# VectorE's share in two more chunks, other parts for chunks 1 and 2, and the transposes of K inside the first PV batch

## The chip, the core and the metric

One core of a Trainium2 chip. The metric is the device time of one launch in microseconds. The kernel before takes 521.86 us (median of three runs, 521.71 to 523.05). For every run the span of the core is known too (first to last counted event of the trace); the time is somewhat longer than the span (by 1.67 us in the profiled run of before). One run of each kernel is profiled.

## The reference

Grouped-query attention with softmax, bf16: 16 batches, 32 query heads, 8 key heads, 288 queries, 512 keys, width 128.

```python
k = jnp.repeat(k, rep, axis=1); v = jnp.repeat(v, rep, axis=1)      # rep = 4
scores = jnp.einsum("bhqd,bhkd->bhqk", q, k) * D ** -0.5
p = softmax(scores); out = jnp.einsum("bhqk,bhkd->bhqd", p, v)
```

## The kernel before

There are 128 groups (batch and key head). The scores of a group, 128 keys x 4608 columns, are cut into three chunks of 1536 columns, 384 chunks in all. TensorE computes the scores of chunk n into one of two PSUM buffers, ScalarE takes exp of them into bf16, and TensorE multiplies by V two chunks later, in a batch of 12 small matmuls (PV); a column of ones in V gives the softmax sum. VectorE takes the reciprocal and evicts. In every sixth chunk VectorE exponentiates 120 of the 1536 columns itself, with a bit trick and a polynomial ("share"). The order on the engines (cut):

```python
FIRST = 2; FIRST_SHARED = 6; EVERY = 6; LAG = 2; TPC = 3

def shared(n):
    return FIRST_SHARED <= n < NS - NC and (n - FIRST_SHARED) % EVERY == 0    # 63 chunks: 6, 12 ... 378

def op_exp(n):                        # ScalarE
    parts = [(0, CH)]
    if shared(n): parts = [(0, CH - W)]                      # 1416 columns
    if n < FIRST or n == NS - 1:
        parts = [(x, x + BANK) for x in range(0, CH, BANK)]  # three times 512
    ...

# TensorE
op_warm(WARM, BANK, ps_o[:, 1]); op_warm(1, P, ps_o[:, 1])   # matmuls on a constant
op_kt(0, range(1), 0); op_kt(0, range(1, NJ), 1)             # K of group 0, transposed
op_warm(1, P, ps_s[:, 1])
for n in range(NS):
    op_s(n)                                                  # scores; wait for K, Q, a free buffer
    if shared(n): op_sy(n)                                   # the 120 columns for VectorE, waits for an eviction
    if n == 2: op_kt(1, range(NJ), 1)                        # K of group 1, transposed
    if n >= LAG: op_pv(n - LAG)

# ScalarE: fetches K of group 1 only when K of group 0 is copied
op_kd(eng, 0); eng.activation(dum[:], ..., ACTF.Exp)
for (s, n) in need(eng, [("s_k0", 2)]): eng.wait_ge(s, n)
op_kd(eng, 1)

# VectorE
op_kc(1, range(NJ), 1, 3)                                    # copies the transposed K; chunk 3 needs it
for r in range(NS - 1):
    n = r + LAG
    op_rc(r)
    if shared(n): op_y(n)
    if shared(n - 1): op_yu(n - 1, 1); op_yu(n - 1, 2); op_yp(n - 1)
    op_ev(r)
    if shared(n): op_yb(n); op_ym(n); op_yu(n, 0)
```

Of the kernel before, what the change touches and what calls it, by code (L numbers as in the profile page):

```python
# [131 lines left out]
def bass_standalone__gqa_softmax__near_ridge_kernel(  # L132
# [13 lines left out]
    NG = B * G  # L146
    assert D == P and Sk % P == 0 and R % P == 0
    BANK = 512
    TPC = 3
    CH = TPC * BANK  # L150
    COLS = NJ * R
    NC = COLS // CH
# [8 lines left out]
    LAG = 2  # L161
    W = 120
    EVERY = 6
# [6 lines left out]
    NQ = 12  # L170
    NPT = 6
    WARM = 5
    FIRST = 2
    FIRST_SHARED = 6
    AHEAD = 1.08
    NO = 12
    NS = NG * NC
    LASTG = NG - 1
    ALONE = 8 * TPC


# [6 lines left out]
    with ExitStack() as es:  # L188
        sem = {}
# [57 lines left out]
        ck_sb = main.enter_context(nc.sbuf_tensor("ck_sb", [P, 3], FP32))  # L247
        bad_sb = main.enter_context(nc.sbuf_tensor("bad_sb", [P, 2, ALONE + 1], FP32))
        y_sb = main.enter_context(nc.sbuf_tensor("y_sb", [P, NB, W], FP32))
# [21 lines left out]
        def emit(eng, waits, fn):  # L271
            waits = need(eng, waits)
            for (s, n) in waits[:-1]:
                eng.wait_ge(s, n)
            ins = fn()
            if waits:
                ins.wait_op(waits[-1][0], waits[-1][1], "sem-ge")
            return ins
# [53 lines left out]
        def op_store(g, i=None):  # L332
            eng = nc.sync
            if i is None:
                for (s, n) in need(eng, [("s_ev", NC * (g + 1))]):
                    eng.wait_ge(s, n)
                eng.dma_start(o_v[g], o_sb[:, g % NO].rearrange("p t d -> p (t d)")).then_inc(
                    sem["s_o%d" % (g % NO) if g < LASTG - 1 else "s_ol"], 16)
            else:
# [6 lines left out]
        def stored():  # L346
            return [("s_o%d" % (g % NO), 16 * (g // NO + 1)) for g in range(NG - NO, LASTG - 1)]

# [21 lines left out]
        def used(i):  # L370

            return max(b for b in range(NC) for t in range(b * TPC, (b + 1) * TPC) for j in range(NJ) if place(t, j)[0] == i)

        def ready(n, x):

            if n < FIRST and x < TPC - 1:
                return ("s_eb", n * (TPC - 1) + x + 1)
            return ("s_e", n + 1 + (x if n == NS - 1 else 0))

        def sequence(b):  # L380

# [17 lines left out]
        def op_kt(g, tiles, bank):  # L399

            eng = nc.tensor
            dst = ps_o[:, bank].bitcast(BF16)
            for x, j in enumerate(tiles):
                ins = emit(eng, [("s_id", 2), ("s_kd%d" % g, 16)], lambda: eng.transpose(  # L404
                    dst[:, x * P:(x + 1) * P], kd_sb[:, g, j * D:(j + 1) * D], ident[:]))
            ins.then_inc(sem["s_kp"], 1)
# [13 lines left out]
        def op_s(n):  # L420
            eng = nc.tensor
            g, i = n // NC, n % NC
            sl, gi = (g // UG) % NSLOT, g % UG
            waits = [have("k", g), have_q(g, i)]
            if n >= 2 + FIRST:
                waits.append(("s_e", n - 1))
            qg = qt_sb[:, g % NQ].rearrange("d t p -> d (t p)")
            todo = pieces(i)
            for x, (c, j, t, w) in enumerate(todo):
                if shared(n) and c + w == CH:  # L430
                    w -= W
                w_x = waits if x == 0 else []
                if n == 0 and x < 2:
                    w_x = [("s_k0", 1), waits[1]] if x == 0 else waits[:1]
                if n == 1 and x < 2:
                    w_x = [have_q(g, x)]
                if 2 <= n < 2 + FIRST:
                    w_x = w_x + [ready(n - 2, c // BANK)]
                ins = emit(eng, w_x, lambda: eng.matmul(  # L439
                    ps_s[:, n % 2, c:c + w], kt_sb[:, sl, j, gi, :], qg[:, t * P:t * P + w], start=True, stop=True))  # L440
                if n < FIRST and (c + w) % BANK == 0 and c + w < CH:
                    ins.then_inc(sem["s_s0"], 1)
            ins.then_inc(sem["s_s"], 1)

# [14 lines left out]
                return ps_s[:, 0, 0:TPC * DV].rearrange("p (a e) -> p a e", e=DV)  # L459
            return ps_o[:, r % 2, 0:TPC * DV].rearrange("p (a e) -> p a e", e=DV)  # L460

        def op_pv(r):
            eng = nc.tensor
            g = r // NC
            sl, gi = (g // UG) % NSLOT, g % UG
            waits = [("s_vc", g + 1)]
            if 2 <= r < NS - 2:
                waits.append(("s_ev", r - 1))
            if r == NS - 2:
                waits.append(("s_e", NS - 1))  # L470


            todo = sequence(r % NC)
            for x, (t, j) in enumerate(todo):
                i, c = place(t, j)
                w_x = (waits if x == 0 else []) + [ready(g * NC + i, c // BANK)]
                if c == CH - P and shared(g * NC + i):
                    w_x.append(("s_yp", nth(g * NC + i)))
                ins = emit(eng, w_x, lambda: eng.matmul(  # L479
                    outs(r)[:, t - r % NC * TPC, :], pt(g, t, j), v_sb[:, sl, gi * NJ + j, 0:DV], start=(x == 0),  # L480
                    stop=(t not in [y[0] for y in todo[x + 1:]]), skip_group_check=True))
            ins.then_inc(sem["s_pv"], 1)

        def op_pv_last():

            eng = nc.tensor
            sl, gi = (LASTG // UG) % NSLOT, LASTG % UG
            for (x, j) in [(x, j) for j in range(NJ) for x in range(TPC - 1)] + [(TPC - 1, j) for j in range(NJ)]:
                t = NT - TPC + x
                i, c = place(t, j)  # L490
                w_x = [ready(LASTG * NC + i, c // BANK)] + ([ready(NS - 1, 0)] if x == TPC - 1 else [])
                ins = emit(eng, w_x, lambda: eng.matmul(
                    outs(NS - 1)[:, x, :], pt(LASTG, t, j),
                    v_sb[:, sl, gi * NJ + j, 0:DV], start=(j == 0), stop=(j == NJ - 1)))
# [3 lines left out]
        def op_exp(n):  # L498
            eng = nc.scalar
            waits = [("s_s", n + 1)]  # L500
            if n >= NPT:
                m = n - NPT
                waits.insert(0, ("s_pv", m // NC * NC + used(m % NC) + 1))
            d, s = pt_sb[:, n % NPT], ps_s[:, n % 2]
            parts = [(0, CH)]
            if shared(n):
                parts = [(0, CH - W)]
            if n < FIRST or n == NS - 1:
                parts = [(x, x + BANK) for x in range(0, CH, BANK)]
            for x, (c, e) in enumerate(parts[:-1]):  # L510
                ins = emit(eng, [("s_s0", (TPC - 1) * n + x + 1)] if n < FIRST else waits, lambda: eng.activation(  # L511
                    d[:, c:e], s[:, c:e], ACTF.Exp, scale=scale))
                ins.then_inc(sem["s_e" if n == NS - 1 else "s_eb"], 1)
            parts = [(d[:, c:e], s[:, c:e]) for (c, e) in parts[-1:]]
            for (d, s) in parts:
                emit(eng, waits, lambda: eng.activation(d, s, ACTF.Exp, scale=scale)).then_inc(sem["s_e"], 1)  # L516


        def shared(n):
            return FIRST_SHARED <= n < NS - NC and (n - FIRST_SHARED) % EVERY == 0  # L520

        def nth(n):
            return (n - FIRST_SHARED) // EVERY + 1

        def op_y(n):
            eng, b = nc.vector, nth(n) % NB
# [63 lines left out]
        def op_ev_last():  # L590

            n, c, t = TPC - 1, TPC * (NS - 1), NT - TPC
            waits = [("s_o%d" % (LASTG % NO), 16 * (LASTG // NO)), ("s_rc", NS)]
            dst, src = o_sb[:, LASTG % NO, t:NT, :], outs(NS - 1)[:, :, 0:D]
# [12 lines left out]
        def op_stat(b):  # L607
            eng = nc.vector
            w = G * NT
            a, e = b * w, (b + 1) * w - (ALONE if b == B - 1 else 0)  # L610
            emit(eng, [("s_rc", e // TPC)], lambda: eng.tensor_reduce(  # L611
# [18 lines left out]
        for u in range(1, NU):  # L630
            t = max(NC * UG * (u - NSLOT + 1) + 0.5, NC * (UG * u - 2.5) / AHEAD - 0.2)
            sp.append((t, lambda u=u: op_k(u)))
            sp.append((t + (2.0 if u >= NSLOT else 0.35), lambda u=u: op_v(u)))
        for g in range(UG, NG):
            t = max(NC * (g - NQ + 1) + 1.2, NC * (g - 2.5) / AHEAD)
# [16 lines left out]
        @block.tensor  # L652
        def _(eng):
            op_warm(WARM, BANK, ps_o[:, 1])
            op_warm(1, P, ps_o[:, 1])
            op_kt(0, range(1), 0)
            op_kt(0, range(1, NJ), 1)
            op_warm(1, P, ps_s[:, 1])
            for n in range(NS):
                op_s(n)  # L660
                if shared(n):
                    op_sy(n)
                if n == 2:
                    op_kt(1, range(NJ), 1)
                if n >= LAG:
                    op_pv(n - LAG)
            op_pv(NS - 2)
            op_pv_last()
            emit(eng, [("s_ev", NS - 2), ("s_bad", 2)], lambda: eng.matmul(  # L669
                ps_o[0:1, NS % 2, 0:ALONE + 1], one_f[:], bad_sb[:, 1, :], start=True, stop=True)  # L670
            ).then_inc(sem["s_bad"], 1)
            choose(eng, "pe")
# [25 lines left out]
        def _(eng):  # L698
# [4 lines left out]
            per_b = G * NC  # L703
            w0 = NS - 1 - ALONE // TPC
            last = rl_sb[:, NG * NT - ALONE:NG * NT]
# [61 lines left out]
```

## Time and profile before

| | before |
|---|---|
| time, span | 521.67 us, 520.0 us (profiled run) |
| TensorE, ScalarE, VectorE, GpSimd busy | 98%, 99%, 71%, 15% |
| a chunk in the steady part | 1.330 us |
| scores of chunk 0, 3, 7 and 383 start at | 4.41, 8.31, 13.76, 513.99 us |

TensorE's matmul records overlap (the three of one chunk's scores at 17.75 fill 0.81 us, and the batch after them starts 0.65 later), so starts are compared here, not busy times. A chunk's pace is the same from chunk 7 to the end. The lines that carry this are in the prediction. In the profile lines, PE is TensorE's matmuls, PEld its weight loads, DVE VectorE, ACT ScalarE and POOL GpSimd.

### The profile page before, as it was taken

The numbers are of one execution on the slowest core, as the hardware profiler recorded it, in microseconds if no ns is written. First come the engines' busy times: TensorE is split into PE (matmuls) and PEld (weight loads), VectorE is DVE, ScalarE is ACT, GpSimd is POOL, SyncE is SP. The second block draws the span as 40 slices with busy tenths as digits, with TensorE's granted clock in tenths as the row PEclk, the third lists the DMA queues.
The fourth block names the chain that finished last, engine by engine and source line by source line (L and its number), as shares of the span: only waits on it lengthen the run. The fifth ranks groups of instructions, "written<-read, shape, count | busy, mean of one in ns | idle before, by whom it ended". The sixth has DMA issues, their size and how long they took to land.

```text
span 520.0 us, 15243 instructions
## 1 busy us (share of the span) xinstructions
PE 510.3 (98%) x6118; PEld 394.6 (76%) x6224; DVE 369.6 (71%) x1315; ACT 513.3 (99%) x393; POOL 79.8 (15%) x135
## 2 busy tenths in 40 slices
PE   8999999999999999999999999999999999999997
PEld 5777777777777777777777777777777777777776
DVE  2767767777777677676776776767767767677776
ACT  7999999999999999999999999999999999999997
POOL 2111111111111111111111111111111111111110
PEclk9999999999999999999999999999999999999999
DMA  9999999999999998999999989999998989998212
GB/s 186 237 218 230 267 194 248 225 213 210 219 233 256 208 245 201 235 248 240 215 241 209 209 225 220 241 185 209 229 240 232 227 194 201 192 234 198 86 69 93
DMA packets 253078, 110.06 MB, mean 212 GB/s; under 512 B 219728, under 2 KB 236752, under 8 KB 253008
## 3 DMA queue, kind: packets, MB, share of 16 engines
q1 hardware_dynamic: 252720, 108.82, 97.7%
q8 instruction: 49, 0.80, 0.7%
q10 hardware_dynamic: 288, 0.26, 0.2%
q14 instruction: 21, 0.17, 0.2%
HBM read 17.04 MB, written 37.75 MB: 105 GB/s over the span
## 4 chain that ended last, share of the span: by engine, by line
ACT 98%; DMA 1%; issue 1%; DVE 0%; PE 0%
ACT pt_sb L516 97%; DMA qt_sb<-in_q_dram 1%; ACT pt_sb L511 1%; PE ps_s L439 0%; DVE o_sb L585 0%; DVE o_sb L595 0%; PE ps_s L479 0%; DVE rl_sb L575 0%; PE ps_o L669 0%; DVE bad_sb L621 0%; DVE flag_i L734 0%; DVE bad_sb L618 0%
## 5 line engine op out<-in xcount | busy, mean ns | idle before, releaser
L516 ACT ACTIVATE pt_sb<-ps_s 128x1536 bf16<-128x1536 f32 (+2 forms) x384 | 508.8, 1441 | 0.0
L479 PE MATMUL ps_o<-v_sb,pt_sb 128*128 128x129 bf16 x4584 | 322.3, 220 | 1.1
L479 PEld LDWEIGHTS ps_o<-v_sb,pt_sb 128*128 128x128 bf16 x4584 | 282.8, 98 | 49.7 <-DVE o_sb L585 14.1
L439 PE MATMUL ps_s<-qt_sb,kt_sb 128*128 128x512 bf16 (+2 forms) x1430 | 290.4, 320 | 5.0 <-DMA qt_sb<-in_q_dram 0.5
L585 DVE TENSOR_TENSOR o_sb<-ps_o,rl_sb 128x384 bf16<-128x384 f32 x382 | 211.9, 555 | 9.3 <-DVE rl_sb L575 0.5
L439 PEld LDWEIGHTS ps_s<-qt_sb,kt_sb 128*128 128x128 bf16 x1536 | 123.9, 98 | 62.3 <-issue 1.1
L575 DVE RECIPROCAL rl_sb<-ps_o 128x3 f32<-128x3 f32 x382 | 68.1, 178 | 125.5 <-PE ps_o L479 124.0
L568 POOL COPY v_sb<-vd_sb 128x512 bf16<-128x512 bf16 x128 | 78.8, 616 | 429.1 <-PE ps_o L479 408.9
L549 DVE SCALAR_TENSOR_TENSOR u_sb<-u_sb,m_sb 128x120 f32<-128x120 f32 x126 | 35.6, 283 | 2.2
L556 DVE SCALAR_TENSOR_TENSOR pt_sb<-u_sb,e_sb 128x120 bf16<-128x120 f32 x63 | 17.8, 283 | 2.2
L549 DVE SCALAR_TENSOR_TENSOR u_sb<-m_sb 128x120 f32<-128x120 f32 x63 | 17.4, 277 | 0.0
L527 DVE TENSOR_SCALAR y_sb<-ps_o 128x120 f32<-128x120 f32 x63 | 15.9, 253 | 0.0
L540 DVE TENSOR_SCALAR m_sb<-t_sb 128x120 int32<-128x120 int32 x63 | 14.1, 223 | 2.2
L540 DVE TENSOR_SCALAR e_sb<-t_sb 128x120 int32<-128x120 int32 x63 | 13.6, 216 | 0.0
L450 PE MATMUL ps_o<-qt_sb,kt_sb 128*128 128x120 bf16 x63 | 13.6, 216 | 0.0
L533 DVE TENSOR_SCALAR t_sb<-y_sb 128x120 int32<-128x120 f32 x63 | 13.4, 213 | 0.0
L450 PEld LDWEIGHTS ps_o<-qt_sb,kt_sb 128*128 128x128 bf16 x63 | 6.2, 98 | 7.4
L511 ACT ACTIVATE pt_sb<-ps_s 128x512 bf16<-128x512 f32 x6 | 3.3, 616 | 2.3 <-PE ps_s L439 2.3
L411 DVE COPY kt_sb<-ps_o 128x128 bf16<-128x128 bf16 (+2 forms) x3 | 1.0, 336 | 6.2 <-PE ps_o L404 6.1
L613 DVE TENSOR_REDUCE st_sb<-rl_sb 128x1 f32<-128x72 f32 (+1 forms) x16 | 3.5, 216 | 0.0
L611 DVE TENSOR_REDUCE st_sb<-rl_sb 128x1 f32<-128x72 f32 (+1 forms) x16 | 3.5, 216 | 0.0
L417 PE MATMUL ps_o<-const-bfloat16-1.0 128*128 128x512 bf16 (+1 forms) x6 | 2.4, 570 | 0.9 <-PEq L752 0.9
(32 smaller groups left out, 12.0 us busy)
## 6 DMA issues: line engine op xcount, KB each, us to landing
out_dram<-o_sb SPq DMA_DIRECT2D x127, 288.0 KB, 3.7
vd_sb<-in_v_dram SPq DMA_DIRECT2D x31, 512.0 KB, 5.5
qt_sb<-in_q_dram SPq DMA_TRANSPOSE x128, 4.9
kt_sb<-in_k_dram SPq DMA_TRANSPOSE x32, 5.1
vd_sb<-in_v_dram SPq DMA_DIRECT2D x1, 384.0 KB, 4.6
out_dram<-o_sb SPq DMA_DIRECT2D x3, 96.0 KB, 1.6
kd_sb<-in_k_dram ACTq DMA_DIRECT2D x2, 128.0 KB, 2.7
vd_sb<-in_v_dram SPq DMA_DIRECT2D x1, 128.0 KB, 3.3
```

What stands on the lines that cost most here:

```text
L439: ins = emit(eng, w_x, lambda: eng.matmul(ps_s[:, n % 2, c:c + w], kt_sb[:, sl, j, gi, :], qg[:, t * P:t * P + w], start=True, stop=True))
L450: emit(eng, [("s_ev", n - LAG - 1)], lambda: eng.matmul(ps_o[:, (n - LAG) % 2, BANK - W:BANK], kt_sb[:, (g // UG) % NSLOT, j, g % UG, :], ...
L479: ins = emit(eng, w_x, lambda: eng.matmul(outs(r)[:, t - r % NC * TPC, :], pt(g, t, j), v_sb[:, sl, gi * NJ + j, 0:DV], start=(x == 0), st ...
L516: emit(eng, waits, lambda: eng.activation(d, s, ACTF.Exp, scale=scale)).then_inc(sem["s_e"], 1)
L527: emit(eng, [("s_yb", nth(n) - NB), ("s_pv", n - LAG + 1)], lambda: eng.tensor_scalar(out=y_sb[:, b], in0=ps_o[:, (n - LAG) % 2, BANK - W: ...
L533: emit(eng, [("s_ym", 2 * (nth(n) - NB)), ("s_y", nth(n))], lambda: eng.tensor_scalar(out=t_sb[:, b], in0=y_sb[:, b], scalar1=Y_MUL, scala ...
L540: emit(eng, [("s_yp", nth(n) - NB), ("s_yb", nth(n))], lambda: eng.tensor_scalar(out=dst[:, b], in0=t_sb[:, b], scalar1=mask, scalar2=bits ...
L549: lambda: eng.scalar_tensor_tensor(out=u_sb[:, b, x], in0=src, scalar=QUARTIC[x], in1=m, op0=ALU.add, op1=ALU.mult)
L556: lambda: eng.scalar_tensor_tensor(out=pt_sb[:, n % NPT, CH - W:CH], in0=u_sb[:, b, 2], scalar=QUARTIC[3], in1=e_sb[:, b].bitcast(FP32), o ...
L568: emit(eng, waits, lambda: eng.tensor_copy(v_sb[:, sl, gi * NJ:(gi + 1) * NJ, 0:D], vd_sb[:, sl, gi].rearrange("p (j d) -> p j d", d=D))). ...
L575: emit(eng, [("s_pv", r + 1)], lambda: eng.reciprocal(rl_sb[:, TPC * r:TPC * (r + 1)].unsqueeze(2), outs(r)[:, :, D:DV])).then_inc(sem["s_ ...
L585: emit(eng, waits, lambda: eng.tensor_tensor(out=o_sb[:, g % NO, t0:t0 + TPC, :], in0=outs(r)[:, :, 0:D], in1=rl_sb[:, TPC * r:TPC * (r + ...
```

## The change

Its intent: relieve ScalarE by two more shares (chunks 3 and 381), let work that depends on part of chunk 2 start sooner, and fill the wait for K of group 1 with PV matmuls.

```diff
-    FIRST = 2
-    FIRST_SHARED = 6
+    FIRST = 3
+    PARTS = {0: (1, 2, 3), 1: (2, 3), 2: (2, 3), NG * NC - 1: (1, 2, 3)}
+    SHARED = [NC] + list(range(2 * NC, NS - NC, EVERY)) + [NS - NC]
 ...
-        def op_pv(r):
+        def op_pv(r, some=slice(None)):
 ...
-            parts = [(x, x + BANK) for x in range(0, CH, BANK)]
+            parts = [(x * BANK, y * BANK) for (x, y) in zip((0,) + PARTS[n], PARTS[n])]
 ...
-            return FIRST_SHARED <= n < NS - NC and (n - FIRST_SHARED) % EVERY == 0
+            return n in SHARED
 ...
                 if n == 2:
+                    op_pv(0, slice(0, TPC * TPC))
                     op_kt(1, range(NJ), 1)
-                if n >= LAG:
+                elif n == 3:
+                    op_pv(0, slice(TPC * TPC, None))
+                    op_pv(1)
+                elif n > 3:
                     op_pv(n - LAG)
```

More of the change, by code (lines that the diff above doesn't have):

```diff
@@ L372, in used, with part, ahead @@
             return max(b for b in range(NC) for t in range(b * TPC, (b + 1) * TPC) for j in range(NJ) if place(t, j)[0] == i)
+        def part(n, x):
+            return sum(x >= e for e in PARTS.get(n, (TPC,)))
+        def ahead(n):
+            return sum(len(PARTS[m]) - 1 for m in range(n))
         def ready(n, x):
-            if n < FIRST and x < TPC - 1:
-                return ("s_eb", n * (TPC - 1) + x + 1)
-            return ("s_e", n + 1 + (x if n == NS - 1 else 0))
+            p = part(n, x)
+            if n < FIRST and p < len(PARTS[n]) - 1:
+                return ("s_eb", ahead(n) + p + 1)
+            return ("s_e", n + 1 + (p if n == NS - 1 else 0))
         def sequence(b):
@@ L440, in op_s @@
                     ps_s[:, n % 2, c:c + w], kt_sb[:, sl, j, gi, :], qg[:, t * P:t * P + w], start=True, stop=True))
-                if n < FIRST and (c + w) % BANK == 0 and c + w < CH:
+                if n < FIRST and (c + w) % BANK == 0 and (c + w) // BANK in PARTS[n][:-1]:
                     ins.then_inc(sem["s_s0"], 1)
@@ L473, in op_pv @@
             todo = sequence(r % NC)
-            for x, (t, j) in enumerate(todo):
+            for x, (t, j) in list(enumerate(todo))[some]:
                 i, c = place(t, j)
@@ L481, in op_pv @@
                     stop=(t not in [y[0] for y in todo[x + 1:]]), skip_group_check=True))
-            ins.then_inc(sem["s_pv"], 1)
+            if x == len(todo) - 1:
+                ins.then_inc(sem["s_pv"], 1)
         def op_pv_last():
@@ L507, in op_exp @@
                 parts = [(0, CH - W)]
-            if n < FIRST or n == NS - 1:
-                parts = [(x, x + BANK) for x in range(0, CH, BANK)]
+            if n in PARTS:
+                parts = [(x * BANK, y * BANK) for (x, y) in zip((0,) + PARTS[n], PARTS[n])]
             for x, (c, e) in enumerate(parts[:-1]):
-                ins = emit(eng, [("s_s0", (TPC - 1) * n + x + 1)] if n < FIRST else waits, lambda: eng.activation(
+                ins = emit(eng, [("s_s0", ahead(n) + x + 1)] if n < FIRST else waits, lambda: eng.activation(
                     d[:, c:e], s[:, c:e], ACTF.Exp, scale=scale))
@@ L519, in shared @@
         def shared(n):
-            return FIRST_SHARED <= n < NS - NC and (n - FIRST_SHARED) % EVERY == 0
+            return n in SHARED
         def nth(n):
-            return (n - FIRST_SHARED) // EVERY + 1
+            return SHARED.index(n) + 1
         def op_y(n):
```

## The prediction

> **What bounds the kernel now.** I read first the busy times and the chain that ended last.
>
> ```profile
> PE 510.3 (98%) x6118; PEld 394.6 (76%) x6224; DVE 369.6 (71%) x1315; ACT 513.3 (99%) x393; POOL 79.8 (15%) x135
> ...
> ACT 98%; DMA 1%; issue 1%; DVE 0%; PE 0%
> ```
>
> TensorE and ScalarE are both full; the chain names ScalarE alone. That would make every column taken off ScalarE a gain, so I checked it with the timeline of ScalarE, one instruction at a time (start, duration), in the steady part. Chunk 12 (1416 columns, VectorE does the other 120) and its neighbours:
>
> ```profile
> 19.95 1.48 ACT L516 ACTIVATE pt_sb<-ps_s 128x1536 bf16<-128x1536 f32 x1
> 21.28 1.39 ACT L516 ACTIVATE pt_sb<-ps_s 128x1416 bf16<-128x1416 f32 x1
> 22.59 1.45 ACT L516 ACTIVATE pt_sb<-ps_s 128x1536 bf16<-128x1536 f32 x1
> 23.94 1.45 ACT L516 ACTIVATE pt_sb<-ps_s 128x1536 bf16<-128x1536 f32 x1
> ```
>
> Ends are 21.43, 22.67, 24.04, 25.39. A backlogged full chunk costs about 1.344 us (ends of chunks 2 to 5: 9.44, 10.78, 12.12, 13.47) and a shared one 1.24. But chunk 13 ends 1.37 after chunk 12: ScalarE had caught up and waited a little for scores, which the records hide because consecutive ones overlap. So in the steady part ScalarE is fed by TensorE. The timeline of TensorE confirms it (L439 scores of a chunk, L479 its PV batch, L450 VectorE's scores):
>
> ```profile
> 17.75 0.81 PE L439 MATMUL ps_s<-qt_sb,kt_sb 128*128 128x512 bf16 x3
> 18.40 0.84 PE L479 MATMUL ps_o<-v_sb,pt_sb 128*128 128x129 bf16 x12
> ...
> 19.73 0.84 PE L479 MATMUL ps_o<-v_sb,pt_sb 128*128 128x129 bf16 x12
> 20.41 0.76 PE L439 MATMUL ps_s<-qt_sb,kt_sb 128*128 128x512 bf16 x3
> 21.01 0.22 PE L450 MATMUL ps_o<-qt_sb,kt_sb 128*128 128x120 bf16 x1
> 21.06 0.84 PE L479 MATMUL ps_o<-v_sb,pt_sb 128*128 128x129 bf16 x12
> 21.74 0.81 PE L439 MATMUL ps_s<-qt_sb,kt_sb 128*128 128x512 bf16 x3
> ```
>
> Scores take 0.65 us, a batch 0.68, and a chunk starts every 1.33, shared or not. Scores of chunk 13 start at 21.74, though the buffer half they need was free at 21.43 (end of chunk 11's exponential): 0.31 of slack. TensorE waits for nobody. From scores of chunk 7 (13.76) to those of 383 (513.99), 376 chunks take 500.23 us, 1.3304 each; ScalarE alone would need (5 x 1.344 + 1.24) / 6 = 1.327. The two are balanced to 0.003 us a chunk, with TensorE the slower. Hence the end is, nearly, the moment at which TensorE's steady run begins plus a constant. The first 14 us decide.
>
> There I read both rows of TensorE, weight loads (PEld) and matmuls (PE):
>
> ```profile
> 7.30 0.23 PEld L404 LDWEIGHTS ps_o<-ident,kd_sb 128*128 128x128 bf16 x4 [0.16 <-DMA kd_sb<-in_k_dram]
> 7.49 0.72 PEld L479 LDWEIGHTS ps_o<-v_sb,pt_sb 128*128 128x128 bf16 x12
> 8.28 0.34 PEld L439 LDWEIGHTS ps_s<-qt_sb,kt_sb 128*128 128x128 bf16 x3
> ...
> 7.31 0.40 PE L404 MATMUL ps_o<-ident,kd_sb 128*128 128x128 bf16 x4
> 7.54 0.84 PE L479 MATMUL ps_o<-v_sb,pt_sb 128*128 128x129 bf16 x12
> 8.31 0.81 PE L439 MATMUL ps_s<-qt_sb,kt_sb 128*128 128x512 bf16 x3
> 8.96 0.94 PE L479 MATMUL ps_o<-v_sb,pt_sb 128*128 128x129 bf16 x12
> ...
> 7.74 0.42 DVE L411 COPY kt_sb<-ps_o 128x512 bf16<-128x512 bf16 x1 [3.51 <-PE ps_o L404]
> ```
>
> The last matmul of the scores of chunk 2 starts at 7.10 and the next could at 7.15; K of group 1 lands at 7.30, so 0.16 is lost. Batch 0 (12 matmuls at 0.056) should be followed at 8.22 but scores of chunk 3 start at 8.31: they wait for VectorE's copy of the transposed K (7.74 to 8.16, seen at 8.28), 0.09 lost. Batch 1 takes 0.77 instead of 0.68, since its weight load at 9.49 waits for the undivided exponential of chunk 2 (end 9.44): 0.09 lost. Batch 4 (13.04 to 13.76) loses 0.04 in the same way to chunk 5 (end 13.47). In all about 0.38 us that a better start could return at most.
>
> [...] this trace has 0.488 for 512 columns and 1.344 for 1536, so 0.836 a column and 0.06 fixed. [...]
>
> **The change, part by part.**
>
> 1. VectorE takes 120 columns of chunks 3 and 381. ScalarE saves 120 x 0.836 = 0.10 us each. TensorE's work hardly changes: 512 columns become 392 + 120 with one more weight load (scores still take 0.65 in the shared chunks above). So this speeds up only the engine that waits. At the tail, scores of chunk 383 are complete at 513.99 + 0.82 = 514.81 and ScalarE starts on them at 514.87. Its backlog then is 0.02 (0.62 for the first 512 columns where 0.60 is the unqueued value), all that can be gained. Against that, VectorE gets ten more instructions just three chunks after chunk 378's; the score matmul of 381 needs the eviction of batch 377 (ends 511.91) and can slip by some 0.05. I count the tail +0.02.
>
> 2. Parts. Chunk 1 goes from 3 x 512 (3 x 0.488 = 1.464) to 1024 + 512 (0.916 + 0.488 = 1.404): -0.06. Chunk 2 goes from 1.344 to 1.404: +0.06. Together nil on ScalarE. But batch 1 and the scores of chunk 4 can begin when two thirds of chunk 2 are done, at about 8.95 instead of 9.44, so the 0.09 in batch 1 goes, if it is still on the path.
>
> 3. The order on TensorE. Before: scores 2, transposes, 12 PV, scores 3, 12 PV. After: scores 2, 9 PV, transposes, scores 3 with VectorE's share, 3 + 12 PV. The intent is to fill the 0.16 spent waiting for K. [...] But nothing now stands between the transposes and the scores that need their copy. Before, transposes at 7.31 led to scores at 8.31, a lag of 1.00: four issues and the last result 0.43, copy 0.42, semaphore and weight load 0.15. The copy chain is the same, so scores 3 start at 7.66 + 0.99 = 8.65, 0.34 later than before. TensorE idles from 7.89 to 8.65, 0.76 us, in place of 0.16 + 0.09.
>
> The sum on TensorE: after scores 3 come 0.65, 15 PV of 0.845, and scores 4 at 8.65 + 1.49 = 10.14, against 9.73 now (+0.41). Exponential 2 is over at about 9.42, so nothing else is waited for. Scores 7 follow at 10.14 + 3 x 1.33 = 14.13, because the 0.04 of batch 4 goes too (ScalarE is no longer behind); now 13.76. So +0.37 at the start of the steady run, +0.02 at the tail: about +0.35 to +0.4 us on 521.86.
>
> **Rivals.**
>
> A. ScalarE is the bound, as the chain of waits says. Then the change gives -0.2 us (two shares) and some more if the start tightens: 521.6. For it: 99% busy and no idle in its row. Against: the steady 1.33 of TensorE through shared chunks, its 0.31 of slack, and the 1.37 after a shared chunk.
>
> B. The copy is quicker than I think, or K landing is later in runs without a profile, so that the reordering pays. If no wait at all were left, scores 7 would start at 7.15 + 0.23 + 4 x 0.65 + 5 x 0.68 = 13.38, 0.38 earlier: 521.5. For it: an author of a tuned kernel would try this for such a gain. Against: the measured chain of 1.00 us has nothing to lie beside, while the wait it removes was 0.16. A middle case would be near no change.
>
> C. The gap makes TensorE drop to half clock for a while. The first four score matmuls, before the warm state, are spaced 0.42 us instead of 0.215. [...] I give it 4%.
>
> D. VectorE, with shares in chunks 3 and 6, delays a PV batch. After chunk 6's share, eviction 5 ends at 16.91 and batch 7 starts on time at 17.07. Eviction of batch 0 now ends just before batch 1's sums are ready, so I expect at most 0.05.
>
> **Range and chances.** The working gives 522.2. I lean 0.1 towards A and B, since I may have missed what the author saw: 522.1. The three runs of before spread over 1.3 us (521.71 to 523.05), so a median can be off by 0.3. Range 521.45 to 522.75: below it B would have to hold in full, above it C. Nothing here is near 2% (10.4 us): faster 0.01, same 0.98, slower 0.01.
>
> **What would show it.** In the changed profile: the transposes of group 1 at about 7.66 without a wait for their DMA; a gap on TensorE of about 0.75 us before the scores of chunk 3, which start near 8.65 after VectorE's copy ends near 8.5; scores 4 near 10.14; exponentials of chunks 4 to 12 with unqueued durations of 1.45 instead of 1.52; a chunk still every 1.330 us; 65 exponentials of 1416 columns; scores of chunk 383 near 514.35. I am wrong if scores 3 start before 8.4, if TensorE's pace in the steady part changes (then ScalarE did bound it), or if matmuls after the gap are spaced 0.42.

The forecast's sum came to +0.37 us at the start of the steady run and +0.02 at the tail, so 0.35 to 0.4 on 521.86, 522.2. One term of it is cut: the start of the transposes at 7.66, from 7.15 and nine PV matmuls, for which no trace shows the figure used. In the trace of before the twelve of batch 0 start 0.0567 us apart; at that, nine take 0.51, which gives 7.66 too, and fifteen 0.85 for the 0.845.

## The result, and the profile after

The changed kernel took 523.51 us (median of four: 524.24, 522.79, 524.02, 523.00) against 521.81 (521.71 to 523.05, four runs). The ratio is 1.0027, 95% interval 1.0004 to 1.005. Ratios here are the mean time of one kernel's fast runs over that of the other's of the same rounds, so not quite the ratio of the medians quoted. Within 2%, as foretold, but outside the range: 1.3 us above the working's 522.2.

First the page of the profiled run (524.24 us, the slowest of the four), busy times and chain:

```profile
span 522.2 us, 15267 instructions
...
PE 511.9 (98%) x6120; PEld 395.7 (76%) x6226; DVE 372.0 (71%) x1331; ACT 513.6 (98%) x393; POOL 79.8 (15%) x135
...
PE 97%; issue 1%; DVE 1%; DMA 1%
```

The chain now names TensorE for 97%, where it named ScalarE for 98%. The steady part still takes 1.33 us a chunk, so the name changed and the pace did not; that ScalarE no longer has a backlog is my reading of it. Rival A, a gain of 0.2 us from two shares, did not come. Then the timeline of TensorE at the start, weight loads first, matmuls after:

```profile
4.49 0.13 PEld L449 LDWEIGHTS ps_s<-qt_sb,kt_sb 128*128 128x128 bf16 x2 [0.76 <-DMA qt_sb<-in_q_dram]
...
6.60 0.15 PEld L449 LDWEIGHTS ps_s<-qt_sb,kt_sb 128*128 128x128 bf16 x1 [0.28 <-issue]
7.03 0.15 PEld L449 LDWEIGHTS ps_s<-qt_sb,kt_sb 128*128 128x128 bf16 x1 [0.28 <-issue]
7.46 0.15 PEld L449 LDWEIGHTS ps_s<-qt_sb,kt_sb 128*128 128x128 bf16 x1 [0.28 <-issue]
...
10.42 0.34 PEld L449 LDWEIGHTS ps_s<-qt_sb,kt_sb 128*128 128x128 bf16 x3 [0.77 <-issue]
...
8.31 1.18 PE L489 MATMUL ps_o<-v_sb,pt_sb 128*128 128x129 bf16 x9
9.29 0.60 PE L414 MATMUL ps_o<-ident,kd_sb 128*128 128x128 bf16 x4
10.45 0.76 PE L449 MATMUL ps_s<-qt_sb,kt_sb 128*128 128x512 bf16 x3 [0.56 <-issue]
```

Weight loads of 512-column matmuls are 0.43 us apart here, twice the 0.215 of the steady part, and each takes 0.15 instead of 0.10; I call this half clock. In the profile before the spacing fell to 0.215 at 6.1 us, and the trace's record of full clock starts at 6.04:

```profile
5.66 0.15 PEld L439 LDWEIGHTS ps_s<-qt_sb,kt_sb 128*128 128x128 bf16 x1 [0.28 <-issue]
6.07 1.07 PEld L439 LDWEIGHTS ps_s<-qt_sb,kt_sb 128*128 128x128 bf16 x7 [0.26 <-issue]
```

Here it is 0.43 until past 7.9, and the nine PV matmuls are 0.108 apart instead of 0.057. Nothing that the change touches runs before 8.2 us on TensorE. The first matmuls at full speed are those after the gap, at 10.45; the clock records in the trace put the step at 9.72.

So this run's scores of chunk 3 start 2.14 us later than before (10.45 against 8.31). Worked out: Q landed 0.09 later; the scores of chunks 0 to 2 took 1.07 longer at half clock; nine PV matmuls were put in between, 0.98 of which 0.51 would be needed at full clock; the wait for K, 0.16, is gone; and transposes to scores took 1.16 instead of 1.00. Sum 0.09 + 1.07 + 0.98 - 0.16 + 0.16 = 2.14. Of this 1.70 is the half clock and 0.35 the order, as I had worked it out. From there to the scores of chunk 383 (516.23, 2.24 later) there is only 0.1 more.

The second surprise lies outside the trace. This run's time exceeds its span by 2.04 us; for the profiled run of before it is 1.67. In all four runs of after it is 2.00 to 2.09.

So the questions were: Is the half clock caused by the change or drawn by lot, is my 0.35 right, and what lengthens the time outside the span?

### The profile page after: what moved, and what is told of

The parts are those of the page before. It is cut to its first block, busy times and chain, and to the rows that moved or that the text cites. A ratio compares the mean times of both kernels' runs of the same rounds, so it can differ in the third digit from the quotient of the medians.

```text
span 522.2 us, 15267 instructions
## 1 busy us (share of the span) xinstructions
PE 511.9 (98%) x6120; PEld 395.7 (76%) x6226; DVE 372.0 (71%) x1331; ACT 513.6 (98%) x393; POOL 79.8 (15%) x135
## 4 chain that ended last, share of the span: by engine, by line
PE 97%; issue 1%; DVE 1%; DMA 1%
PE ps_o L489 50%; PE ps_s L449 46%; DMA qt_sb<-in_q_dram 1%; PE ps_o L460 1%; DVE o_sb L596 0%; DVE u_sb L560 0%; DVE rl_sb L586 0%; DVE o_sb L606 0%; PE ps_o L414 0%; DVE pt_sb L567 0%; DVE t_sb L544 0%; PE ps_o L684 0%; DVE m_sb L551 0%; DVE bad_sb L632 0%; DVE flag_i L749 0%
## 5 line engine op out<-in xcount | busy, mean ns | idle before, releaser
L560 DVE SCALAR_TENSOR_TENSOR u_sb<-u_sb,m_sb 128x120 f32<-128x120 f32 x130 | 36.8, 283 | 2.3
L522 ACT ACTIVATE pt_sb<-ps_s 128x512 bf16<-128x512 f32 (+1 forms) x6 | 4.2, 740 | 2.5 <-PE ps_s L449 2.4
```

What stands on the lines that cost most here:

```text
L560: lambda: eng.scalar_tensor_tensor(out=u_sb[:, b, x], in0=src, scalar=QUARTIC[x], in1=m, op0=ALU.add, op1=ALU.mult)
```

## The experiments

The kernel before was run again with each call, 47 times; with its first four runs that makes 51, medians 521.70 to 522.68 by call, extremes 521.51 and 523.05. A run of before is thus itself uncertain by over 1 us. "Outside" below is time minus span. Before has 1.65 to 1.75 in all 47 of these runs.

### First call: the two kernels again, and the reordering by itself

before_again: no edit.

> The kernel before, unchanged. Theory W (TensorE's step from half to full clock comes at a moment that varies from run to run, whatever the kernel): its ten or so times fall into more than one group, most near 521.8 and some near 523; if the profile catches a late one, score matmuls spaced 0.42 us go on past 6.1 us from the start. Theory O (the late step is caused by the new order): all times lie within 521.6 to 522.1 but for rare ones, and the profile shows the step at about 6.1.

Measured: 522.45 (522.00 to 523.01), ratio 0.9998 (0.9984 to 1.0012). The profile shows a third start: full clock already at the first scores (seven weight loads from 4.47 on within 1.19 us), but K of group 1 late. Weight loads of TensorE:

```profile
8.49 0.23 PEld L404 LDWEIGHTS ps_o<-ident,kd_sb 128*128 128x128 bf16 x4 [1.73 <-DMA kd_sb<-in_k_dram]
```

K landed 4.1 us after its issue at 4.31, where the profile of before had 3.0. In the start of the unchanged kernel two things thus differ from run to run, which I call lots: the step of the clock and the landing of K.

after_again: no edit.

> The changed kernel, unchanged. Theory W: times in groups, the early ones near 522.2 (my 0.36 for the reordered transposes), the late ones 1.2 to 1.8 higher; the profile, whichever it catches, shows a gap of 0.75 to 1.1 us before the scores of chunk 3. Theory O: no time below 522.7, the step of the clock always after 9 us.

Measured: 522.99 (522.05 to 523.73), ratio 1.0007 (0.9994 to 1.0021). One time at 522.05 refutes theory O as I had put it. The clock stepped at 9.15, just before the transposes (9.21); scores of chunk 3 at 10.17, a lag of 0.96 from the transposes.

only_kt: before with the reordering alone (cut: `op_pv` takes a slice, as in the change).

```diff
                 if n == 2:
+                    op_pv(0, slice(0, TPC * TPC))
                     op_kt(1, range(NJ), 1)
-                if n >= LAG:
+                elif n == 3:
+                    op_pv(0, slice(TPC * TPC, None)); op_pv(1)
+                elif n > 3:
                     op_pv(n - LAG)
```

> The kernel before with the reordering alone (nine PV matmuls, transposes of group 1, scores of chunk 3, the other PV matmuls); no shares, no new parts. W with my sum: early times near 522.2 (+0.4), late ones above 523. Theory O: all near 523.3, as the changed kernel. A third, S (the shares or the parts cost it): 521.8, as before.

Measured: 522.78 (522.08 to 524.58), ratio 1.0000 (0.9986 to 1.0013). Its profiled run, the slowest of all at 524.58, shows rival C, to which I had given 4%. Weight loads of TensorE:

```profile
6.66 0.55 PEld L479 LDWEIGHTS ps_o<-v_sb,pt_sb 128*128 128x128 bf16 x9
8.64 0.23 PEld L404 LDWEIGHTS ps_o<-ident,kd_sb 128*128 128x128 bf16 x4 [1.43 <-DMA kd_sb<-in_k_dram]
9.58 0.34 PEld L439 LDWEIGHTS ps_s<-qt_sb,kt_sb 128*128 128x128 bf16 x3 [0.71 <-issue]
...
11.95 0.15 PEld L439 LDWEIGHTS ps_s<-qt_sb,kt_sb 128*128 128x128 bf16 x1 [0.28 <-issue]
12.37 0.15 PEld L479 LDWEIGHTS ps_o<-v_sb,pt_sb 128*128 128x128 bf16 x1 [0.28 <-issue]
```

The clock was full from the first scores (seven weight loads from 4.42 on within 1.19 us), K was late, TensorE idled 1.43 and then, because of the new order, 0.71 us more; from 10.6 to 14.0, 3.4 us, it ran at half clock again (loads 0.11 and 0.43 apart). before_again had the same early clock and late K (wait 1.73), but not the second gap, and did not fall back. One run each, so a case, not a rate.

The traces keep records of the granted clock. From its first step to its end after the last matmul the full clock lasts 515.41 us in the profiled run of before and 512.00 in that of after, 3.41 apart. Over all 20 profiles its length is a whole number of times 3.413 us, 149 to 152, except here: 2 times, then once at half clock (10.64 to 14.06), then 149. The first steps come anywhere from 3.75 to 10.02 us. What sets these lengths and moments is not shown. My estimate from the records and from the spacing of 0.43 against 0.215: a step that comes 3.41 us later costs a busy TensorE up to half of that, 1.7 us, about what the profiled run of after lost.

no_kt: after, with the transposes in front of the first batch again.

```diff
                 if n == 2:
-                    op_pv(0, slice(0, TPC * TPC))
                     op_kt(1, range(NJ), 1)
-                elif n == 3: ...
+                if n >= LAG:
                     op_pv(n - LAG)
```

> The changed kernel with the transposes back in front of the first PV batch; shares and parts kept. W: early times 521.6 to 521.8 (batch 1 and batch 4 lose their 0.09 and 0.04), some late ones near 523. O: 521.7, never late. S: 523, as the changed kernel.

Measured: 522.55 (522.17 to 523.55), ratio 0.9998 (0.9984 to 1.0011). Its profiled run had half clock until 10.0, without the reordering. So a late step came without the new gap and the new order: theory W in that. Outside: 1.74 to 2.05, as after, while only_kt has 1.65 to 1.68.

### Second call: the lot of the clock taken away

All kernels with _fill in their name, and kd_first, have this edit. Five more small matmuls occupy TensorE from 3.9 to 4.3 us, when it waited for Q:

```diff
             op_kt(0, range(1, NJ), 1)
-            op_warm(1, P, ps_s[:, 1])
+            op_warm(6, P, ps_s[:, 1])
```

before_fill:

> The kernel before with six instead of one small warm-up matmuls in the gap of TensorE ahead of the first scores (3.9 to 4.4 us), nothing else. Theory W (part of the spread is the moment at which the clock steps up[...]): the profile shows score matmuls spaced 0.215 us from the first or second chunk on, and the runs lose their late group; what spread is left (521.7 to 522.7) comes from the landing of K of group 1, between 7.3 and 8.6 us so far. If filling does nothing to the step, matmuls at 0.43 us go on past 6 us as often as before.

Measured: 521.91, and all five runs within 521.81 to 522.00 (the nine of before on the same chip: 521.64 to 522.74); ratio 0.9997 (0.9983 to 1.001). The step came at 6.2 to 6.4. In all 14 filled kernels it came between 4.4 and 7.1 and no profile shows a fall-back, while three of the six unfilled profiles had it at 9.15 or later. My "first or second chunk" was too early in some, but the late group is gone. Why matmuls in that gap go with an early step is not shown.

after_fill:

> The changed kernel with the same six warm-up matmuls. Theory R (the reordering costs a fixed chain: the transposes lead to the scores of chunk 3 a full 1.0 us later, with nothing beside it): scores of chunk 3 start 0.95 to 1.0 us after the transposes; where K lands early (7.3) the kernel is 0.35 slower than before_fill, where it lands late (8.5) about the same, so mean 0.1 to 0.4 us slower than before_fill. Theory C (what made the first measurement +1.4 was the clock, through the gap): then it is equal or lower once filled, unless the profile shows matmuls spaced 0.11 us again after the gap, as the run with the reordering alone did from 10.6 to 14.0 us.

Measured: 522.31 (522.22 to 522.56), ratio 1.0006 (0.9992 to 1.0019) against before, +0.40 us to before_fill: medians of the span 520.5 against 520.2, outside 1.84 against 1.72. So 0.3 of the change lies in the span and 0.1 outside. Matmuls of its profile:

```profile
7.04 0.67 PE L489 MATMUL ps_o<-v_sb,pt_sb 128*128 128x129 bf16 x9
7.72 0.40 PE L414 MATMUL ps_o<-ident,kd_sb 128*128 128x128 bf16 x4
8.68 0.76 PE L449 MATMUL ps_s<-qt_sb,kt_sb 128*128 128x512 bf16 x3 [0.56 <-issue]
9.27 0.21 PE L460 MATMUL ps_o<-qt_sb,kt_sb 128*128 128x120 bf16 x1
9.33 1.01 PE L489 MATMUL ps_o<-v_sb,pt_sb 128*128 128x129 bf16 x15
```

Transposes to scores 0.96, and nothing beside them. The last transpose is issued by 7.9 and the scores follow at 8.68: the gap of nearly 0.8 that I had drawn.

before_fill_k and after_fill_k: K of group 1 asked for earlier.

```diff
-            for (s, n) in need(eng, [("s_k0", 2)]):
+            for (s, n) in need(eng, [("s_kd0", 16)]):
                 eng.wait_ge(s, n)
             op_kd(eng, 1)
```

> before_fill, and K of group 1 is fetched as soon as K of group 0 has landed (about 3.2 us) instead of after its copies (about 4.3). It should land 1 us earlier, at 6.3 to 7.5, so that the transposes wait little or nothing: 521.2 to 521.7, with a narrow spread, if theory R and W are right. If the landing is limited by the other transfers in flight it stays near 7.3 to 8.5 and the time as before_fill.

> The changed order with both. Theory R: K lands before the nine PV matmuls end, so nothing but the chain is left: 0.35 us slower than before_fill_k, scores of chunk 3 about 1.0 us after the transposes. If the order is not the cause: equal to before_fill_k or 0.1 faster through shares and parts.

Measured: 522.19 (521.82 to 522.81) and 522.45 (522.01 to 522.74), ratios 1.0002 and 1.0006. The edit failed: issued 1 us earlier (3.3 and 3.2), K took 4.8 and 4.3 us to land, so at 8.1 and 7.5, no earlier than otherwise. Whether the other transfers in flight set the landing is not shown. The difference of the two, 0.26, has the sign of the chain but proves little.

### Third call: the parts of the change, each on the filled kernel

only_kt_fill (the edit of only_kt):

> Filled kernel before with the reordering alone. Theory R (the chain transposes, copy, scores of chunk 3 lies bare): span 520.4 to 520.6 against 520.1 to 520.2 of before_fill, and the time outside the span stays at 1.7 us as in all kernels without shares: 522.2 to 522.3. Rival S: if the 0.4 us between after_fill and before_fill came from shares or parts, it is 521.9 like before_fill.

Measured: 522.19 (521.95 to 522.39), span 520.3 to 520.7, outside 1.65 to 1.75, ratio 1.0006 (0.9992 to 1.002).

no_kt_fill (the edit of no_kt):

> Filled, shares and parts, the old order. Theory R: span 520.0 to 520.1 (the waits in batches 1 and 4 go, 0.1 at most). The time outside the span, 1.7 us in every kernel without shares and 1.75 to 2.09 in every one with them, should be 1.8 to 2.0: 521.9 to 522.1. Rival S: 522.3 with a span of 520.4.

Measured: 522.51 (522.38 to 522.82), span 520.3 to 520.8, outside 2.00 to 2.08, ratio 1.0013 (0.9999 to 1.0027). The span is 0.4 longer than theory R allowed: shares or parts cost it, and without the reordering.

shares_fill:

```diff
+    SHARED = [NC] + list(range(2 * NC, NS - NC, EVERY)) + [NS - NC]
-            return FIRST_SHARED <= n < NS - NC and (n - FIRST_SHARED) % EVERY == 0
+            return n in SHARED
```

> Filled kernel before with the two shares alone. If the time outside the span comes with the shares (24 more instructions, ten of them near the end): span 520.1 to 520.2, outside it 1.8 to 2.0, time 521.9 to 522.2. If it comes with the parts: 1.7 outside, time 521.8 to 521.9.

Measured: 522.31 (521.81 to 522.60), span 520.1 to 520.7, outside 1.71 to 2.11, ratio 1.0009 (0.9995 to 1.0022).

parts_fill (no_kt_fill with the 63 old shares):

> Filled kernel before with the new parts of chunks 1 and 2 alone. Mirror of the last: 1.7 us outside the span and 521.8 to 521.9 if the shares bring it; 1.8 to 2.0 outside if the parts do. Span 520.1 (the 0.09 of batch 1 goes where scores of chunk 3 start early enough to reach it).

Measured: 521.73 (521.70 to 522.00), span 519.9 to 520.3, outside 1.70 to 1.80, ratio 1.0001 (0.9987 to 1.0015). The parts cost and bring nothing that shows; the shares, meant to relieve ScalarE, are what is left for both pieces. The times alone don't settle it (the interval of shares_fill holds 1), so the traces have to. Where in the span? TensorE's matmul for the share of chunk 6, in no_kt_fill:

```profile
12.79 0.76 PE L449 MATMUL ps_s<-qt_sb,kt_sb 128*128 128x512 bf16 x3
13.90 0.23 PE L460 MATMUL ps_o<-qt_sb,kt_sb 128*128 128x120 bf16 x1 [0.35 <-DVE o_sb L596]
```

It should follow its scores after 0.6 us (13.39) and comes 0.5 later, waiting for VectorE's eviction. In shares_fill it came 0.25 late (13.60 for 13.35). VectorE was late with chunk 3's share, and the timeline of VectorE and GpSimd of the same run says why:

```profile
11.06 0.49 DVE L544 TENSOR_SCALAR t_sb<-y_sb 128x120 int32<-128x120 f32 x1
11.59 0.52 DVE L551 TENSOR_SCALAR m_sb<-t_sb 128x120 int32<-128x120 int32 x1
12.03 0.21 DVE L551 TENSOR_SCALAR e_sb<-t_sb 128x120 int32<-128x120 int32 x1
...
10.87 1.17 POOL L579 COPY v_sb<-vd_sb 128x512 bf16<-128x512 bf16 x2 [4.50 <-DMA vd_sb<-in_v_dram]
```

Two instructions of 0.22 took 0.49 and 0.52 while GpSimd copied V (10.87 to 12.04); the next, after the copies, took 0.21 again. Each time 0.27 to 0.3 us were lost; shares_fill has one such step (0.52 us). Not every instruction of VectorE is slower beside a copy: in the profiled run of before 126 evictions beside copies of V took 0.55 us (median) and the 256 others 0.56. Why these steps were slower is not shown.

### Fourth call: which share brings which piece

share3_fill (list without 381):

> Filled kernel before, chunk 3 shared in addition, 381 not. If the share of chunk 3, so close to that of chunk 6, holds up VectorE: TensorE's matmul for chunk 6's share starts 0.25 to 0.5 us late, span 520.3 to 520.5 against 520.15; time outside the span 1.7; time 522.0 to 522.2. If chunk 3 is innocent: span 520.1, 521.8.

Measured: 522.06 (521.66 to 522.96, six runs), span 520.0 to 521.3, outside 1.66 to 1.75, ratio 1.0003. In the profiled run (span 520.0) V landed earlier, GpSimd was through by 10.94, and the share's integer steps started just then:

```profile
10.79 0.22 DVE L533 TENSOR_SCALAR t_sb<-y_sb 128x120 int32<-128x120 f32 x1
...
9.77 1.17 POOL L568 COPY v_sb<-vd_sb 128x512 bf16<-128x512 bf16 x2 [3.83 <-DMA vd_sb<-in_v_dram]
```

No delay, chunk 6's matmul on time at 13.12. The collision is a third lot: of the 20 profiles, three show it (no_kt_fill, shares_fill, and swap_fill below), all of kernels that share chunk 3.

share381_fill (list without 3):

> Filled kernel before, chunk 381 shared in addition, 3 not. If the piece outside the span comes from 381: outside 1.9 to 2.1, span 520.1 to 520.2, time 522.1; the store of group 126 is issued near 516.3 instead of 515.3, with the three last ones bunched behind it. If it does not come from 381: 1.7 outside, 521.8.

Measured: 522.16 (521.91 to 523.20), span 520.2 to 521.5 (the profiled run waited 1.67 us for K, without a fall-back of the clock), ratio 0.9998. Outside 1.66 to 1.72: not this share. Its stores were bunched as expected (group 126 at 517.42, the last three at 518.17, 518.82 and 519.37), and it cost nothing outside.

ev_first_fill:

```diff
+                if n - 1 == NS - NC: op_ev(r)
                 if shared(n - 1): op_yu(n - 1, 1); op_yu(n - 1, 2); op_yp(n - 1)
-                op_ev(r)
+                if n - 1 != NS - NC: op_ev(r)
```

> share381_fill, but at the end VectorE evicts batch 380 before it finishes its share of chunk 381 (same instructions, other order). If the outer piece comes from late, bunched stores: outside the span 1.7 again, 521.8 to 521.9. If it comes from the number of instructions or anything else of the share: 1.9 to 2.1, 522.1.

Measured: 522.04 (521.71 to 522.17), span 520.0 to 520.4, outside 1.71 to 1.79, ratio 0.9995. It had nothing to mend, because share381_fill already had its stores bunched and nothing more outside; that run is what my theory of late stores falls by.

kd_first: parts_fill, K of group 1 right behind K of group 0.

```diff
             op_kd(eng, 0)
+            op_kd(eng, 1)
             eng.activation(dum[:], ...)
-            for (s, n) in need(eng, [("s_k0", 2)]): eng.wait_ge(s, n)
-            op_kd(eng, 1)
```

> The new parts alone (parts_fill), with K of group 1 fetched right behind K of group 0 at the very start. It should land by 4.5, so that no kernel waits for it: scores of chunk 3 near 8.1 instead of 8.55, 521.3 to 521.5. If it holds up K of group 0 or Q of group 0 (4.36) the first scores start later by that much and the gain is gone: 521.7 or more.

Measured: 522.43 (522.25 to 523.77, six runs), ratio 1.0012 (0.9998 to 1.0026). No wait for K (it landed at 4.75), but Q of group 0 came late; first scores 0.9 later than in parts_fill:

```profile
5.33 2.95 PE L449 MATMUL ps_s<-qt_sb,kt_sb 128*128 128x512 bf16 x12 [0.62 <-DMA qt_sb<-in_q_dram]
```

### Fifth call: the time outside the span

Only both shares together lengthened it. What they add beyond one is length: 1331 counted instructions on VectorE against 1323 and 1315.

swap_fill: shares_fill without chunks 192 and 252.

```diff
-    SHARED = [NC] + list(range(2 * NC, NS - NC, EVERY)) + [NS - NC]
+    SHARED = [NC] + [n for n in range(2 * NC, NS - NC, EVERY) if n not in (192, 252)] + [NS - NC]
```

> Filled kernel before, chunks 3 and 381 shared, chunks 192 and 252 no longer (63 shares, instruction counts as before). If the length of a stream decides: outside the span 1.7 us. If the pair of shares decides: 1.9 to 2.1. Span 520.1 to 520.5, the higher where GpSimd's copies of V fall on VectorE's integer steps for chunk 3 and hold up the score matmul of chunk 6; time 521.8 to 522.2.

Measured: 522.42 (522.02 to 522.66), span 520.3 to 520.9, outside 1.72 to 1.80, ratio 1.0006. The same collision with GpSimd is in its profile (0.55 us for one step, GpSimd from 10.27 to 11.44), but the outer piece is gone although both shares are there.

pad_fill:

```diff
             eng.memset(one_f[:], 1.0)
+            for x in range(20):
+                eng.memset(pad_sb[:, x:x + 1], 0.0)
```

> Filled kernel before with 20 tiny memsets more on VectorE at its start, when it has nothing to do (0.9 to 3.5 us), on a tensor that nobody reads. If the length of VectorE's stream decides: outside the span 1.9 to 2.1, span 520.1 as before_fill, 522.1. If the length of TensorE's stream or the pair of shares decides: 1.7 outside, 521.85.

Measured: 522.04 (522.04 to 522.30), span 520.1 to 520.4, outside 1.84 to 2.02, ratio 1.0001. Twenty idle instructions early on VectorE, no new share, and the time outside the span grows by 0.1 to 0.3. So the length of VectorE's stream brings it. The DMA records that the traces keep past the span show more. After the end of the span, the profiled run of after has one packet of 8 KB on an instruction queue, and that of before has none (`--dma` of 522.5 to 525 and of 520.2 to 523 us):

```profile
DMA packets 1, 0.01 MB, mean 3 GB/s; under 512 B 0, under 2 KB 0, under 8 KB 0
q14 instruction: 1, 0.01, 1.4%
...
DMA packets 0, 0.00 MB, mean 0 GB/s; under 512 B 0, under 2 KB 0, under 8 KB 0
```

All eight profiles with 1331 or 1335 instructions on VectorE have this packet, 1.8 us after the end of the span; none of the twelve with 1315 or 1323 has it. It takes 0.32 to 0.58 us, and its end is the last thing in each of these traces, 2.15 to 2.40 after the span. Where it is missing, the trace ends 2.01 to 2.07 after the span. In all 20 profiled runs the end of the trace lies 0.32 to 0.33 us further behind the span than the measured time does, so this late packet accounts for the whole piece, in its size too. Why it comes with the longer stream is not shown.

## Why the prediction was wrong

The measured 523.51 is 1.65 above the 521.86 that I started from; I had 0.35 to 0.4. Point by point:

1. **The bound.** Right. TensorE sets the steady pace: 1.33 us a chunk in every kernel, and between the two profiled runs nothing but 0.1 us changed from chunk 3's to chunk 383's scores. Relieving ScalarE brought nothing, so rival A is out.
2. **The chain transposes, copy, scores 3.** Right in mechanism and size: lag 0.95 to 0.96 at full clock (0.99 predicted), gap 0.8, and +0.35 in the breakdown of the profiled run. In the span after_fill has +0.3 (its shares included), only_kt_fill +0.3 to before_fill (another chip) and +0.5 to parts_fill (the same chip). My starting point, K landing at 7.30, was only one draw: K landed between 7.3 and 8.9. When it is late, both orders wait for it and the reordering should cost less. Rival B counted on such late landings; no run shows a gain from them.
3. **Rival C, half clock for a while, "I give it 4%".** This is the step that failed most. I read the start of before from one profile and took its step at 6.1 us as fixed, so my sum began with 7.15, the moment at which TensorE has issued chunk 2's scores at that clock. In the profiled run of after that moment is 8.31. The step is drawn anew in each run: 3.75, 3.82, 6.04, 9.15, 9.72 and 10.02 in the six unfilled profiles. In the profiled run of after it is 1.70 of the 2.57 us between the two profiled runs (the rest: 0.35 the order, 0.37 outside the span, 0.1 after chunk 3's scores, 0.09 a later Q). It is not caused by the change in that run, where half clock came before anything new; in only_kt the new gap did precede a fall-back of 3.4 us. Whether the changed kernel draws badly more often is likely but not shown: its nine unfilled runs average 523.3 and its five filled ones 522.3, for before 522.2 (51 runs) and 521.9.
4. **Rival D, "I expect at most 0.05".** Mis-sized. I placed VectorE's share of chunk 3 by TensorE and VectorE alone and forgot GpSimd's copies of V, which run just then in some runs: 0.25 in shares_fill and 0.5 us in no_kt_fill on the path. The profiled run of after was spared: its late scores put the share's integer steps (12.87) behind the copies (12.17 to 12.79). What the other runs had is open.
5. **The tail, "+0.02".** The sum had no term for the time outside the span. It is 0.3 in the first four runs of after (2.00 to 2.09 against 1.7). It comes with the length of VectorE's stream (1.84 to 2.02 in pad_fill, with twenty instructions more), as one late packet on an instruction queue.
6. **The parts** nil, as worked out.

So on one footing the terms are about +0.3 for the order (more on one chip), +0.1 to 0.3 outside the span, 0 to 0.5 for chunk 3's share, and the lot of the clock on top. My range was built from the spread of three runs, and missed that a start at half clock alone moves a run by over 1 us. No version is clear of noise below the kernel before: the lowest ratio, 0.9995 of ev_first_fill, has the interval 0.9982 to 1.0008. Filling the gap ahead of the first scores only makes the time steadier (521.81 to 522.00 in before_fill, where before had 521.64 to 522.74 on the same chip).

## What to carry to other kernels

Before you price a change of a few tenths of a microsecond in the start of a kernel, look at several profiles of the unchanged kernel: the step of the clock (here anywhere from 3.75 to 10.02 us without the fill) and the landing of the first transfers (K here at 7.3 to 8.9) differ from run to run, and one profile shows only one draw. Work moved in front of a chain of transpose, copy and use can delay that chain, if nothing is left to lie beside it (here by 0.35 us: nine PV matmuls of 0.51 in front, 0.16 of waiting gone). Before giving an off-path engine more work, check what the other engines do at that moment, not only how idle it is on average (here steps of 0.22 us took 0.49 to 0.55 beside GpSimd's copies).
